# A fused attention and mixer kernel: some score products in plain fp32, without split q and k, and a new order of steps

## Chip, cores and metric

The kernel runs on one core of one Trainium2 chip. The metric is the device time of one execution in microseconds. Its engines are TensorE (matrix products and transposes), VectorE, ScalarE, GpSimd, and SyncE, which issues the loads; they run side by side, each in the order of its own instructions, and wait for each other by semaphores. In the profile they are PE (PEld for the loading of a product's stationary operand), DVE, ACT, POOL and SP.

## What is computed

Three parts in a row, all in fp32: causal attention over 2 batches of 12 heads (448 positions, head dimension 64), a mixer over positions and channels, and a block with a two-dimensional Fourier transform, a normalization and a two-layer product.

```python
scores = np.matmul(q, k.transpose(0, 1, 3, 2)) / np.sqrt(64)
scores = np.where(np.triu(ones, k=1), -1e9, scores)
attn = np.exp(scores - scores.max(-1, keepdims=True))
attn = attn / (attn.sum(-1, keepdims=True) + 1e-9)
x = merge_heads(np.matmul(attn, v))                      # (2, 448, 768)
u = x + (np.maximum(x.T @ w_tok1, 0) @ w_tok2).T         # over positions
x = u + np.maximum(u @ w_ch1, 0) @ w_ch2                 # over channels
u = x + np.real(np.fft.fft(np.fft.fft(x, axis=1), axis=2))
out = u + np.maximum(normalize(u) @ m2_ch1, 0) @ m2_ch2
```

## The kernel before

**Precision.** Most products multiply numbers that are split in two: a value rounded to the short form fp32r ("high") and the rest ("low"). A product of two split operands is three passes of fp32r, high by high, high by low, low by high. Transposes and the product of P with V are in plain fp32, which TensorE does as two instructions for each product.

**Attention.** The 24 heads are worked in 12 pairs; pair n holds two heads on partitions 0 to 63 and 64 to 127, and the two products of a pair (e = 0 and 1) use one half of the array's rows each. The 448 query rows are 4 blocks of 112; block i needs only the first 112 (i + 1) keys, and the widths were rounded up to 256 at least. Blocks 0 and 1 of a pair share a group (g = 0), blocks 2 and 3 are the groups 1 and 2. After a group's products, four small bf16 products add the causal mask (-1e9 above the diagonal).

**Steps and engines.** `ORDER` is a list of words; each word is one step, and the order of the words is the order of the instructions on every engine, so a word's place decides what stands ahead of it in its own engine's queue. Nothing is reordered at run time: a step that waits holds all later steps of its engine. The letters (pair n, and a part after a point):

- K: the loads of raw k and q (SyncE, two each); V: load of v; R: load of a raw weight (float64 words).
- k, l: kh and kl, the split of k (ScalarE; GpSimd, for pair 0 VectorE). q, m: qh (q times 0.125, ScalarE) and ql (VectorE).
- S n.g: score products of a group with its masks (TensorE). N n.i: the negated row maxima (nmx, VectorE). E n.i: the exponentials, two activations, each with a read of the row sum (ScalarE).
- T n.u: the transposes of P (TensorE), C n.u: their copy out of PSUM (pt; ScalarE for u = 1 and 3, else VectorE); P: P times V; O: its copy (ScalarE); X: transposes back (TensorE).
- Z: row sum plus 1e-9 and its reciprocal (`divisors`, VectorE, tiles of 112 x 8); x: the division (VectorE). h, g: the split of the result (ScalarE, GpSimd).
- A, r, s and D, d: the mixer over positions for three pairs at a time; B, b: transposes of x and their copy; u, w: the split of the result.
- W k.j: step j of converting raw weight k; W0 and W1 are w_tok1 (tiles w1h, w1l) and w_tok2, step 5 is the subtraction for the low part on GpSimd. U, y, z, Y, a: the first channel products.

**Buffers.** PSUM has 8 banks. Banks 0 to 3 are the ring of `ybank` (transposes, P times V, mixer), banks 4 to 7 are two pairs for scores (`spair`). A step that takes a bank waits until the last readers of what was in it are done. Raw q and k are loaded into tiles of `resid` that are free at this time, 6 of them for the first 5 pairs, later 3 (`stage`); a load waits until the last reader of the tile is done.

**Start.** Seven products of a constant with itself (`mean_w`) keep TensorE working until the first scores.

Of the kernel before, what the change touches and what calls it, by code (L numbers as in the profile page):

```python
# [70 lines left out]
ORDER = """K0 k0 l0 K1 q0 m0 S0.0 N0.0 N0.1 S0.1 N0.2 S0.2 k1 l1 N0.3 q1 m1 E0.0 E0.1 S1.0 N1.0 N1.1 K2 E0.2 S1.1 E0.3 T0.2 T0.0
N1.2 C0.2 k2 q2 E1.0 T0.1 T0.3 C0.0 T0.4 E1.1 l2 m2 S1.2 E1.2 S2.0 N1.3 V1 V0 C0.3 N2.0 C0.4 C0.1 P0 R0 W0.0 W0.1 N2.1
K3 K4 E1.3 k3 T1.0 T1.2 S2.1 T1.1 C1.0 O0 T1.4 T1.3 C1.2 X0 E2.0 q3 E2.1 N2.2 E2.2 S2.2 l3 m3 S3.0 C1.1 k4 Z0 x0 N2.3
C1.3 q4 C1.4 P1 N3.0 E2.3 T2.0 T2.3 T2.4 N3.1 S3.1 R1 W1.0 O1 T2.2 W0.2 m4 C2.0 B0.0 C2.3 T2.1 C2.4 X1 E3.0 E3.1 S3.2
N3.2 E3.2 l4 S4.0 V3 V2 b0.0 C2.1 C2.2 P2 W0.3 W0.4 W0.5 N3.3 N4.0 Z1 x1 N4.1 K5 q5 E3.3 T3.0 C3.0 T3.1 T3.2 Z2 O2
T3.4 k5 C3.2 C3.1 B0.1 X2 T3.3 E4.0 E4.1 S4.1 S4.2 C3.4 W1.1 b0.1 h0 C3.3 P3 l5 g0 N4.2 N4.3 E4.2 m5 S5.0 E4.3 S5.1 x2
T4.3 Z4 W1.2 Z3 T4.4 C4.4 O3 h1 T4.1 h2 T4.0 C4.3 T4.2 C4.0 C4.2 N5.0 X3 K6 C4.1 k6 N5.2 N5.1 B0.2 g2 g1 R2 W2.0 q6
A0.1 A0.0 x3 V5 V4 W1.3 W2.1 E5.0 E5.1 S5.2 l6 m6 E5.2 S6.0 W1.4 K7 r0.0 N5.3 P4 E5.3 S6.1 N6.0 N6.1 s0.0 r0.1 b0.2
T5.4 O4 k7 s0.1 X4 T5.1 T5.0 C5.4 T5.2 E6.0 E6.1 x4 W1.5 D0.0 C5.1 D0.1 N6.2 C5.0 T5.3 W2.2 S6.2 E6.2 q7 h3 l7 m7 S7.0
d0.1 C5.2 K8 q8 C5.3 P5 N6.3 R3 k8 h4 N7.0 E6.3 N7.1 d0.0 T6.4 T6.2 T6.0 E7.0 E7.1 S7.1 S7.2 O5 T6.3 l8 g4 V6 K9 C6.3  # L80
k9 C6.2 C6.4 B1.1 X5 C6.0 T6.1 D0.2 N7.2 m8 q9 Z5 x5 N7.3 W2.3 b1.1 B1.2 C6.1 B1.0 P6 Z6 d0.2 E7.2 S8.0 N8.0 N8.1 h5
E7.3 T7.3 O6 b1.2 T7.0 b1.0 T7.2 C7.3 T7.4 T7.1 C7.0 X6 E8.0 E8.1 S8.1 S8.2 C7.1 W2.4 Z7 g5 g3 C7.2 A1.1 C7.4 A1.0 x6
N8.2 B2.0 N8.3 W3.0 W3.1 W3.2 E8.2 l9 m9 S9.0 E8.3 S9.1 V7 P7 V8 K10 r1.1 s1.1 u0.1 h6 W2.5 Z8 u0.0 r1.0 s1.0 N9.0
T8.0 W3.3 T8.1 b2.0 T8.3 q10 u0.2 k10 R4 W4.0 N9.1 E9.0 O7 X7 C8.1 C8.0 T8.4 E9.1 C8.3 D1.0 x7 B2.1 T8.2 N9.2 S9.2 m10
E9.2 l10 w0.1 S10.0 C8.4 d1.0 C8.2 P8 b2.1 N9.3 E9.3 T9.2 T9.1 D1.1 W3.4 O8 h7 K11 q11 T9.0 W4.1 N10.0 N10.1 W4.2 C9.2
T9.3 C9.1 T9.4 E10.0 C9.3 E10.1 d1.1 X8 C9.0 D1.2 S10.1 S10.2 m11 x8 h8 k11 C9.4 V9 P9 V11 Z9 u1.0 N10.2 E10.2 N10.3
E10.3 d1.2 O9 W3.5 l11 S11.0 S11.1 B2.2 R5 W5.0 b2.2 T10.1 C10.1 T10.0 T10.2 g7 g8 w0.2 w0.0 g6 N11.0 N11.2 N11.1
T10.3 C10.3 u1.2 E11.0 A2.0 r2.0 C10.2 C10.0 X9 T10.4 W4.3 A2.1 W5.1 x9 W5.2 W4.4 E11.1 S11.2 s2.0 V10 C10.4 P10 N11.3
u1.1 E11.2 r2.1 s2.1 E11.3 T11.2 C11.2 T11.0 C11.0 T11.1 O10 T11.4 T11.3 W5.3 C11.4 X10 W4.5 R6 W6.0 W6.1 Z10 R7 C11.1
C11.3 P11 w1.2 D2.0 O11 X11 x10 D2.2 d2.2 Z11 x11 h10 d2.0 B3.1 b3.1 u2.0 h9 W5.4 w1.1 w1.0 U0 g10 B3.2 U1 W6.2 u2.2  # L90
y0 b3.2 h11 B3.0 y1 W5.5 W7.0 W7.1 W6.3 W6.4 g9 g11 A3.0 A3.1 z0 D2.1 b3.0 r3.0 s3.0 W7.2 z1 W7.3 r3.1 s3.1 U2 y2 D3.0
D3.1 d3.0 z2 d3.1 W7.4 U3 D3.2 y3 u3.1 W6.5 W7.5 w2.2 w2.0 d2.1 u3.0 u2.1 w3.0 w3.1 w2.1 z3 Y0 a0 d3.2 Y1 a1 u3.2 w3.2
"""


# [5 lines left out]
def fused_kernel(ctx: ExitStack, tc: tile.TileContext, qk, v, w1, w2, wa, wb, wc, wd, fa, fb, out):  # L101
# [159 lines left out]
    with ExitStack() as actx:  # L261
# [94 lines left out]
        def maxima(n, i):  # L356
            c = pairs[n]
            if i == 0:
                c.nmx = small(ap, "nmx")
# [2 lines left out]
            if n or g < 2:
                vec.tensor_reduce(  # L363
                    out=c.nmx[:, i], in_=c.sp[g][:TS, :, c0 : c0 + w], axis=AX.X, op=ALU.max, negate=True
                )
            else:
                for e in range(2):
                    vec.tensor_reduce(out=c.nmx[:, i, e], in_=c.se[g][e][:, :w], axis=AX.X, op=ALU.max, negate=True)
# [641 lines left out]
```

## Time and profile before

| | us |
|---|---|
| median of 3 runs | 685.57 |
| fastest and slowest run | 685.55, 686.62 |
| span of the profiled execution | 687.0 |
| busy in it: TensorE, VectorE, ScalarE, GpSimd | 680.4, 534.8, 291.7, 125.5 |

The profile is of one more execution, whose own time is its span, from the first instruction to the last. A row of a time line gives start, length, engine, line, operation, the tiles written and read, shapes, how many instructions were merged into it, and in brackets the idle time before it with what ended it. Lengths of matrix products are modelled and overlap; the distance from one start to the next says what a product really costs.

### The profile page before, as it was taken

To read this page: it belongs to the slowest core of one execution; us is meant where nothing else is said; L and a number is where in the kernel's file an instruction comes from. 1 tells how busy PE (TensorE), PEld (TensorE's weight loads), DVE (VectorE), ACT (ScalarE), POOL (GpSimd) and SP (SyncE) were. 2 spreads that over 40 slices of the span, in tenths; PEclk is the share of its full clock that TensorE was granted. 3 is DMA by queue.
4 is the path that set the end of the run, shared out by engine and by line. 5 is a ranking of instruction groups with operands and counts; after the bars stand their busy time and mean duration, and the time that the engine had idled before them with its cause. 6 is when DMAs were issued, how large, how long until landed. Compare 5 with 4: busy or idle time off the path is not lost.

```text
span 687.0 us, 10288 instructions
## 1 busy us (share of the span) xinstructions
PE 680.4 (99%) x3946; PEld 623.8 (91%) x3946; DVE 534.8 (78%) x885; ACT 291.7 (42%) x624; POOL 125.5 (18%) x106
## 2 busy tenths in 40 slices
...
GB/s 268 68 103 138 91 99 45 49 234 151 125 127 133 111 149 95 93 1 1 92 77 108 123 144 76 120 92 153 93 122 93 155 124 151 93 84 83 108 48 54
...
## 3 DMA queue, kind: packets, MB, share of 16 engines
...
q14 instruction: 18, 0.15, 0.1%
HBM read 69.96 MB, written 2.75 MB: 106 GB/s over the span
## 4 chain that ended last, share of the span: by engine, by line
PE 98%; DVE 1%; DMA 0%; ACT 0%; issue 0%; DVEq 0%
PE psum L247 13%; PE psum L226 13%; PE psum L227 13%; PE psum L252 13%; PE psum L251 13%; PE psum L228 12%; PE psum L340 4%; PE psum L391 4%; PE psum L408 3%; PE psum L472 2%; PE psum L503 2%; PE psum L701 2%; PE psum L770 1%; PE psum L354 1%; PE psum L427 1%; PE psum L490 1%
## 5 line engine op out<-in xcount | busy, mean ns | idle before, releaser
L247 PE MATMUL psum<-gh,wh 128*128 128x448 f32 x432 | 157.4, 364 | 0.0
L226 PE MATMUL psum<-acth,wh 128*128 128x448 f32 x432 | 156.9, 363 | 0.0
L252 PE MATMUL psum<-gl,wh 128*128 128x448 f32 x432 | 156.5, 362 | 0.0
L227 PE MATMUL psum<-acth,wl 128*128 128x448 f32 x432 | 156.4, 362 | 0.0
L251 PE MATMUL psum<-gh,wl 128*128 128x448 f32 x432 | 156.1, 361 | 0.0
L228 PE MATMUL psum<-actl,wh 128*128 128x448 f32 x432 | 155.9, 361 | 0.0
L141 ACT ACTIVATE m<-w 128x512 f32<-128x512 f32 (+2 forms) x92 | 71.0, 773 | 127.4 <-DVE wl L161 83.0
L159 ACT CAST wh<-m 128x512 fp32r<-128x512 f32 (+1 forms) x90 | 63.4, 705 | 91.6 <-PE psum L252 52.1
L252 PEld LDWEIGHTS psum<-gl,wh 128*128 128x128 f32 x432 | 81.0, 188 | 6.4 <-DVE gl L234 0.4
L226 PEld LDWEIGHTS psum<-acth,wh 128*128 128x128 f32 x432 | 81.1, 188 | 5.7
L228 PEld LDWEIGHTS psum<-actl,wh 128*128 128x128 f32 x432 | 80.9, 187 | 5.8
L251 PEld LDWEIGHTS psum<-gh,wl 128*128 128x128 f32 x432 | 80.9, 187 | 5.5 <-issue 0.2
L247 PEld LDWEIGHTS psum<-gh,wh 128*128 128x128 f32 x432 | 81.1, 188 | 5.2 <-issue 0.2
L227 PEld LDWEIGHTS psum<-acth,wl 128*128 128x128 f32 x432 | 81.0, 188 | 4.6
L161 DVE TENSOR_TENSOR wl<-m,wh 128x512 fp32r<-128x512 f32 (+1 forms) x84 | 69.5, 830 | 14.3 <-ACT wh L159 13.9
L143 DVE TENSOR_SCALAR m<-m 128x512 f32<-128x512 f32 (+2 forms) x92 | 49.9, 543 | 38.8 <-ACT m L141 38.3
L148 DVE SCALAR_TENSOR_TENSOR m<-w,m 128x512 uint32<-128x512 uint32 (+2 forms) x92 | 78.5, 853 | 2.1
L152 DVE SCALAR_TENSOR_TENSOR m<-w,m 128x512 uint32<-128x512 uint32 (+2 forms) x92 | 78.2, 850 | 2.0
L232 ACT ACTIVATE gh<-psum 128x448 fp32r<-128x448 f32 x72 | 37.7, 540 | 65.0 <-PE psum L228 64.8
L234 DVE SCALAR_TENSOR_TENSOR gl<-psum,gh 128x448 fp32r<-128x448 f32 x72 | 43.8, 619 | 26.0 <-ACT gh L232 26.0
L378 ACT ACTIVATE p<-psum,nmx 112x112 f32<-112x112 f32 (+3 forms) x96 | 46.5, 503 | 10.6 <-DVE nmx L363 9.4
L144 DVE TENSOR_SCALAR m<-m 128x512 uint32<-128x512 uint32 (+2 forms) x92 | 48.0, 522 | 2.4
...
## 6 DMA issues: line engine op xcount, KB each, us to landing
...
```

The lines of the kernel that those rows point to most:

```text
L141: act.activation(out=m, in_=hi.bitcast(F32), func=AF.Abs)
L143: vec.tensor_scalar(out=m, in0=m, scalar1=F64_MIN, scalar2=F64_MAX, op0=ALU.max, op1=ALU.min)
L148: vec.scalar_tensor_tensor(out=mu, in0=lo, scalar=29, in1=mu, op0=ALU.logical_shift_right, op1=ALU.bitwise_or)
L152: vec.scalar_tensor_tensor(out=mu, in0=hi, scalar=0xC0000000, in1=mu, op0=ALU.bitwise_and, op1=ALU.bitwise_or)
L159: act.copy(wh, m)
L161: low_engine[0].tensor_tensor(out=wl, in0=m, in1=f(wh), op=ALU.subtract)
L226: mm(pb[:, :S], lhsT=lh, rhs=act_h[ct][b], start=ct == 0, stop=False)
L227: mm(pb[:, :S], lhsT=ll, rhs=act_h[ct][b], start=False, stop=False)
L228: tail[0] = mm(pb[:, :S], lhsT=lh, rhs=act_l[ct][b], start=False, stop=ct == NCT - 1).ins
L247: mm(pb[:, :S], lhsT=lh, rhs=gh, start=j + k == 0 and seeded is None, stop=False, skip_group_check=seeded is not None,)
L251: mm(pb[:, :S], lhsT=ll, rhs=gh, start=False, stop=False, skip_group_check=seeded is not None)
L252: tail[0] = mm(pb[:, :S], lhsT=lh, rhs=gl, start=False, stop=j == last and k == nk - 1, skip_group_check=seeded is not None,).ins
```

## The change

1. For pairs 0 and 1, all score products are plain fp32, from the raw k and from q scaled by 0.125 in place on VectorE (step e, two halves of 224 columns each; part 0 serves blocks 0 and 1). Steps k, l, q and m of these pairs are gone, and their widths are no longer rounded up to 256. Raw q is loaded ahead of k.
2. For pairs 2 to 11, block 0 alone is plain fp32 on 112 columns, from raw k and from a scaled copy of q's first 112 columns (q0, a new step e on GpSimd). Blocks 1 to 3 stay three passes.
3. S0.2 and S1.0 take two neighbouring banks of the `ybank` ring (`ypair`); the maxima of S0.2 become one reduction.
4. The addition in `divisors` becomes a `scalar_tensor_tensor` whose two inputs are both ssum.
5. The warm-up products read a constant 1.0 from the program's own constants; the tile `ones` is smaller.
6. `ORDER` is new throughout.

```diff
-ORDER = """K0 k0 l0 K1 q0 m0 S0.0 N0.0 N0.1 S0.1 N0.2 S0.2 k1 l1 N0.3 q1 m1 E0.0 E0.1 S1.0 N1.0 N1.1 K2 E0.2 S1.1 E0.3 T0.2 T0.0
-N1.2 C0.2 k2 q2 E1.0 T0.1 T0.3 C0.0 T0.4 E1.1 l2 m2 S1.2 E1.2 S2.0 N1.3 V1 V0 C0.3 N2.0 C0.4 C0.1 P0 R0 W0.0 W0.1 N2.1
...
-N3.2 E3.2 l4 S4.0 V3 V2 b0.0 C2.1 C2.2 P2 W0.3 W0.4 W0.5 N3.3 N4.0 Z1 x1 N4.1 K5 q5 E3.3 T3.0 C3.0 T3.1 T3.2 Z2 O2
...
+ORDER = """K0 e0.0 K1 e0.1 e1.0 S0.0 N0.0 N0.1 K2 S0.1 e1.1 S0.2 E0.0 N0.2 S1.0 E0.1 S1.1 E0.2 N1.0 q2 N0.3
+m2 S1.2 N1.2 k2 V1 K3 N1.1 E0.3 E1.2 l2 T0.2 e2 C0.2 Z0 E1.0 T0.4 E1.1 S2.0 V0 T0.0 N1.3 C0.4 E1.3 T0.3 T0.1
+T1.0 C0.0 C0.1 N2.0 C0.3 T1.2 q3 N2.1 K4 E2.1 S2.1 R0 N2.2 P0 E2.0 C1.0 k3 T1.4 Z1 m3 E2.2 C1.2 S2.2 O0 C1.4
...
+C4.2 T4.1 S5.2 C4.0 K6 C4.4 W0.5 h2 C4.3 N5.2 q6 k6 g2 l6 m6 Z3 E5.2 W1.0 V4 C4.1 N5.3 E5.3 B0.1 e6 A0.1 X3
+Z4 W1.1 b0.1 W1.2 W1.3 K7 r0.1 k7 S6.0 P4 A0.0 O4 W1.4 s0.1 B0.2 x3 W1.5 e7 T5.2 l7 q7 N6.1 r0.0 s0.0 T5.1
...
-    ones = const.tile([1, 128], F32, name="ones")
+    ones = const.tile([1, 16], F32, name="ones")
...
+    warm = nc.const_aps.tensor(1.0, [128, 128], F32)
     for _ in range(7):
-        mm(psum[:, 7, :128], lhsT=mean_w, rhs=mean_w, start=True, stop=True)
+        mm(psum[:, 7, :128], lhsT=warm, rhs=warm, start=True, stop=True)
...
+    def ypair():
+        turn["y"] += turn["y"] % 2
+        k = take("y", 4)
+        take("y", 4)
+        return psum[:, k : k + 2]
...
-            c.k32, c.q32 = stage(n), stage(n)
-            nc.sync.dma_start(out=c.k32, in_=qk[b, hp, :, 1])
-            nc.sync.dma_start(out=c.q32, in_=qk[b, hp, :, 0])
+            c.q32, c.k32 = stage(n), stage(n)
+            for t, part in ((c.k32, 1), (c.q32, 0)) if n >= 2 else ((c.q32, 0), (c.k32, 1)):
+                nc.sync.dma_start(out=t, in_=qk[b, hp, :, part])
...
+        def q_first(n, part=0):
+            c = pairs[n]
+            if n < 2:
+                cols = c.q32[:, 2 * TS * part : 2 * TS * (part + 1)]
+                vec.tensor_scalar(out=cols, in0=cols, scalar1=0.125, scalar2=None, op0=ALU.mult)
+                return
+            c.q0 = a1.tile([128, TS], F32, tag="q0", name="q0")
+            pool.tensor_scalar(out=c.q0, in0=c.q32[:, :TS], scalar1=0.125, scalar2=None, op0=ALU.mult)
...
-            if n or g < 2:
-                sp = c.sp[g] = spair()
-                se = c.se[g] = [sp[:TS, e] for e in range(2)]
-            else:
-                se = c.se[g] = [ybank()[:TS] for e in range(2)]
+            sp = c.sp[g] = ypair() if (n, g) in ((0, 2), (1, 0)) else spair()
+            se = c.se[g] = [sp[:TS, e] for e in range(2)]
             for i, c0 in BLOCKS[g]:
-                w = max(256, TS * (i + 1))
-                for m, (qt, kt) in enumerate(((c.qh, c.kh), (c.qh, c.kl), (c.ql, c.kh))):
+                w = max(256 if n >= 2 and i else 0, TS * (i + 1))
+                if n < 2 or i == 0:
+                    passes = ((c.q32 if n < 2 else c.q0, c.k32),)
+                else:
+                    passes = (c.qh, c.kh), (c.qh, c.kl), (c.ql, c.kh)
+                for m, (qt, kt) in enumerate(passes):
...
-            vec.tensor_scalar(out=c.ssum, in0=c.ssum, scalar1=1.0e-9, scalar2=None, op0=ALU.add)
+            vec.scalar_tensor_tensor(out=c.ssum, in0=c.ssum, scalar=1.0e-9, in1=c.ssum, op0=ALU.add, op1=ALU.max)
```

## Rows read from the trace of the kernel before

**Rows 1.** The page: span, and busy time of each engine

```profile
span 687.0 us, 10288 instructions
...
PE 680.4 (99%) x3946; PEld 623.8 (91%) x3946; DVE 534.8 (78%) x885; ACT 291.7 (42%) x624; POOL 125.5 (18%) x106
```

**Rows 2.** Table of stretches: start and end, length, busy time (instructions) by engine

```profile
core 0: us, PE busy (x) PEld busy (x) DVE busy (x) ACT busy (x) POOL busy (x), PEclk, DMA share, GB/s
...
8.00:12.00 4.00, 3.35 (x22) 2.44 (x22) 2.52 (x4) 4.00 (x17) 0.00 (x0) 1.00 1.03 288
...
26.70:34.36 7.66, 7.66 (x82) 6.00 (x81) 7.56 (x12) 7.66 (x24) 0.98 (x1) 1.00 0.41 122
...
119.46:150.00 30.54, 30.54 (x169) 27.83 (x169) 13.46 (x29) 12.45 (x26) 10.73 (x11) 1.00 0.47 157
```

**Rows 3.** Time line of TensorE, 4 to 20 us

```profile
4.54 0.55 PE L340 MATMUL psum<-kh,qh 64*112 64x256 f32 x2
...
5.69 0.41 PE L340 MATMUL psum<-kh,qh 64*112 64x256 f32 x2
...
6.33 0.57 PE L354 MATMUL psum<-maskb,identb 56*112 56x224 bf16 x4
6.59 0.60 PE L340 MATMUL psum<-kh,qh 64*112 64x336 f32 x2
...
11.11 0.56 PE L340 MATMUL psum<-kh,ql 64*112 64x256 f32 x2 [0.65 <-DVE ql L317]
...
13.64 3.90 PE L391 MATMUL psum<-ident,p 112*112 112x112 f32 x20
...
18.25 0.37 PE L340 MATMUL psum<-kh,qh 64*112 64x256 f32 x2
...
19.32 2.11 PE L408 MATMUL psum<-pt,v 112*64 112x448 f32 x16
```

**Rows 4.** Time line of TensorE, 34 to 48 us

```profile
34.36 2.11 PE L408 MATMUL psum<-pt,v 112*64 112x448 f32 x16
36.40 0.98 PE L391 MATMUL psum<-ident,p 112*112 112x112 f32 x8
38.30 0.98 PE L391 MATMUL psum<-ident,p 112*112 112x112 f32 x8 [0.93 <-DVE x L440]
...
44.72 0.28 PE L340 MATMUL psum<-kh,qh 64*112 64x256 f32 x2
...
45.07 0.35 PE L354 MATMUL psum<-maskb,identb 56*112 56x224 bf16 x4
...
45.93 2.13 PE L391 MATMUL psum<-ident,p 112*112 112x112 f32 x20
```

**Rows 5.** Time line of VectorE, near 35 and near 97 us

```profile
35.01 2.27 DVE L420 TENSOR_SCALAR ssum<-ssum 112x8 f32<-112x8 f32 x1
...
97.01 0.95 DVE L148 SCALAR_TENSOR_TENSOR m<-w,m 128x768 uint32<-128x768 uint32 x1
```

**Rows 6.** The instructions of line L420: shortest, median, longest in ns

```profile
L420 DVE TENSOR_SCALAR ssum<-ssum x12: 161/165/2274, 24.6 to 125.2; 112x8 f32<-112x8 f32 x12
```

**Rows 7.** Time line of GpSimd, near 35 and near 97 us

```profile
34.89 2.37 POOL L161 TENSOR_TENSOR w1l<-m,w1h 112x1024 fp32r<-112x1024 f32 x1 [7.20 <-ACT w1h L159]
...
97.38 2.30 POOL L161 TENSOR_TENSOR wl<-m,wh 128x768 fp32r<-128x768 f32 x1 [7.66 <-PE psum L391]
```

**Rows 8.** Groups by line and shape: busy time, mean ns of one, idle before

```profile
L313 ACT ACTIVATE qh<-resid 128x448 fp32r<-128x448 f32 x12 | 7.1, 590 | 0.9 <-PE psum L340 0.9
...
L317 DVE SCALAR_TENSOR_TENSOR ql<-resid,qh 128x448 fp32r<-128x448 f32 x12 | 7.4, 617 | 0.3 <-ACT qh L313 0.3
...
L308 POOL TENSOR_TENSOR kl<-resid,kh 128x448 fp32r<-128x448 f32 x11 | 12.7, 1155 | 34.9 <-ACT kh L304 34.9
```

**Rows 9.** Landing of the second and third load, issued at 1.18 and 1.65

```profile
DMA to landing us min/median/max: 2.7/2.7/2.7
...
DMA to landing us min/median/max: 4.0/4.0/4.0
```

More of the change, by code (lines that the diff above doesn't have):

```diff
@@ L68 @@
 ENGINES = {getattr(mybir.EngineType, e) for e in ("PE", "DVE", "Activation", "Pool", "SP")}
-ORDER = """K0 k0 l0 K1 q0 m0 S0.0 N0.0 N0.1 S0.1 N0.2 S0.2 k1 l1 N0.3 q1 m1 E0.0 E0.1 S1.0 N1.0 N1.1 K2 E0.2 S1.1 E0.3 T0.2 T0.0
-N1.2 C0.2 k2 q2 E1.0 T0.1 T0.3 C0.0 T0.4 E1.1 l2 m2 S1.2 E1.2 S2.0 N1.3 V1 V0 C0.3 N2.0 C0.4 C0.1 P0 R0 W0.0 W0.1 N2.1
-K3 K4 E1.3 k3 T1.0 T1.2 S2.1 T1.1 C1.0 O0 T1.4 T1.3 C1.2 X0 E2.0 q3 E2.1 N2.2 E2.2 S2.2 l3 m3 S3.0 C1.1 k4 Z0 x0 N2.3
-C1.3 q4 C1.4 P1 N3.0 E2.3 T2.0 T2.3 T2.4 N3.1 S3.1 R1 W1.0 O1 T2.2 W0.2 m4 C2.0 B0.0 C2.3 T2.1 C2.4 X1 E3.0 E3.1 S3.2
@@ L75 @@
-N3.2 E3.2 l4 S4.0 V3 V2 b0.0 C2.1 C2.2 P2 W0.3 W0.4 W0.5 N3.3 N4.0 Z1 x1 N4.1 K5 q5 E3.3 T3.0 C3.0 T3.1 T3.2 Z2 O2
[L76 to L89, printed above, removed]
@@ L90 @@
-C11.3 P11 w1.2 D2.0 O11 X11 x10 D2.2 d2.2 Z11 x11 h10 d2.0 B3.1 b3.1 u2.0 h9 W5.4 w1.1 w1.0 U0 g10 B3.2 U1 W6.2 u2.2
-y0 b3.2 h11 B3.0 y1 W5.5 W7.0 W7.1 W6.3 W6.4 g9 g11 A3.0 A3.1 z0 D2.1 b3.0 r3.0 s3.0 W7.2 z1 W7.3 r3.1 s3.1 U2 y2 D3.0
-D3.1 d3.0 z2 d3.1 W7.4 U3 D3.2 y3 u3.1 W6.5 W7.5 w2.2 w2.0 d2.1 u3.0 u2.1 w3.0 w3.1 w2.1 z3 Y0 a0 d3.2 Y1 a1 u3.2 w3.2
+ORDER = """K0 e0.0 K1 e0.1 e1.0 S0.0 N0.0 N0.1 K2 S0.1 e1.1 S0.2 E0.0 N0.2 S1.0 E0.1 S1.1 E0.2 N1.0 q2 N0.3
+m2 S1.2 N1.2 k2 V1 K3 N1.1 E0.3 E1.2 l2 T0.2 e2 C0.2 Z0 E1.0 T0.4 E1.1 S2.0 V0 T0.0 N1.3 C0.4 E1.3 T0.3 T0.1
@@ new lines @@
+T1.0 C0.0 C0.1 N2.0 C0.3 T1.2 q3 N2.1 K4 E2.1 S2.1 R0 N2.2 P0 E2.0 C1.0 k3 T1.4 Z1 m3 E2.2 C1.2 S2.2 O0 C1.4
+l3 V3 T1.1 T1.3 N2.3 q4 C1.1 m4 X0 e3 S3.0 x0 R1 C1.3 W0.0 N3.0 E2.3 P1 e4 T2.2 S3.1 N3.1 T2.1 E3.1 O1 T2.0
+W0.1 E3.0 B0.0 C2.2 S3.2 k4 N3.2 C2.0 K5 l4 W0.2 N3.3 V2 T2.4 C2.1 T2.3 E3.2 X1 b0.0 C2.3 S4.0 C2.4 N4.0 q5
+E3.3 k5 l5 P2 S4.1 T3.0 x1 E4.0 T3.2 O2 T3.1 N4.1 W0.3 N4.2 V5 C3.0 X2 E4.1 C3.2 h0 E4.2 S4.2 C3.1 m5 Z2
+T3.3 C3.3 T3.4 e5 h1 C3.4 S5.0 g0 N4.3 W0.4 E4.3 P3 g1 O3 x2 T4.2 N5.1 E5.1 T4.0 N5.0 T4.3 R2 S5.1 E5.0 T4.4
@@ new lines @@
+C4.2 T4.1 S5.2 C4.0 K6 C4.4 W0.5 h2 C4.3 N5.2 q6 k6 g2 l6 m6 Z3 E5.2 W1.0 V4 C4.1 N5.3 E5.3 B0.1 e6 A0.1 X3
+Z4 W1.1 b0.1 W1.2 W1.3 K7 r0.1 k7 S6.0 P4 A0.0 O4 W1.4 s0.1 B0.2 x3 W1.5 e7 T5.2 l7 q7 N6.1 r0.0 s0.0 T5.1
+N6.0 b0.2 S6.1 m7 T5.3 C5.1 D0.0 C5.2 T5.0 Z5 E6.0 E6.1 K8 N6.2 E6.2 C5.3 d0.0 S6.2 D0.2 N6.3 C5.0 E6.3 T5.4
+q8 X4 S7.2 d0.2 S7.0 k8 C5.4 x4 D0.1 N7.3 T6.0 T6.4 W2.0 P5 N7.0 V6 m8 d0.1 l8 N7.1 T6.3 E7.3 S7.1 h3 h4
+C6.0 W2.1 E7.1 O5 C6.4 e8 T6.1 E7.0 C6.3 C6.1 N7.2 R3 g3 T6.2 E7.2 W2.2 B1.1 S8.2 X5 g4 C6.2 x5 K9 q9 N8.3
@@ new lines @@
+k9 b1.1 h5 P6 E8.3 e9 O6 T7.0 m9 W3.0 S8.1 T7.3 W2.3 g5 C7.0 S8.0 T7.2 N8.2 C7.3 E8.2 B1.2 A1.0 N8.0 T7.1 l9
+C7.2 N8.1 K10 S9.0 r1.0 b1.2 E8.1 C7.1 W3.1 W3.2 s1.0 B1.0 X6 V7 b1.0 N9.0 A1.1 E8.0 S9.1 u0.1 N9.1 Z6 T7.4
+e10 x6 E9.0 C7.4 r1.1 E9.1 W2.4 w0.1 s1.1 W2.5 R4 T8.0 Z7 P7 T8.3 q10 D1.0 Z8 k10 m10 C8.3 C8.0 W3.3 S9.2 O7
+W3.4 X7 B2.0 V8 W4.0 N9.2 d1.0 E9.2 b2.0 D1.2 N9.3 l10 T8.2 E9.3 S10.0 x7 u0.0 T8.4 T8.1 h7 d1.2 D1.1 K11
+k11 N10.1 Z9 q11 C8.1 C8.4 u0.2 l11 w0.2 C8.2 E10.1 N10.0 W3.5 g7 m11 R5 S10.2 h6 T9.0 P8 T9.1 u1.2 d1.1
@@ new lines @@
+E10.0 N10.3 V9 S10.1 C9.0 T9.2 V11 O8 C9.2 E10.3 X8 C9.1 T9.4 x8 S11.1 B2.1 e11 C9.4 N10.2 T9.3 w0.0 h8 w1.2
+C9.3 P9 E10.2 T10.0 b2.1 N11.2 u1.1 T10.1 T10.2 O9 W4.1 C10.0 T10.4 E11.2 S11.0 C10.1 T10.3 S11.2 C10.4 u1.0
+V10 g8 W5.0 C10.2 N11.0 E11.0 W4.2 B2.2 g6 W4.3 Z10 C10.3 N11.1 A2.0 N11.3 E11.1 w1.1 r2.0 W5.1 b2.2 X9 W4.4
+A2.1 r2.1 W5.2 s2.0 w1.0 E11.3 U0 P10 x9 s2.1 R6 W5.3 T11.0 T11.3 O10 T11.2 C11.0 T11.4 X10 C11.3 C11.2 x10
+y0 Z11 T11.1 C11.1 W4.5 W6.0 z0 W5.4 R7 W6.1 D2.2 U2 C11.4 W5.5 P11 W6.2 W7.0 B3.1 d2.2 D2.0 W7.1 D2.1 h10
@@ L93 @@
+W6.3 O11 g10 W6.4 y2 W6.5 X11 z2 h9 b3.1 U1 d2.0 x11 U3 h11 W7.2 d2.1 B3.0 y1 u2.2 y3 z1 g9 g11 A3.1 u2.1
+u2.0 A3.0 b3.0 w2.1 W7.3 B3.2 w2.0 W7.4 W7.5 r3.0 z3 Y0 r3.1 s3.1 b3.2 s3.0 D3.0 d3.0 D3.2 u3.0 d3.2 a0 w3.0
+D3.1 u3.2 w2.2 d3.1 w3.2 u3.1 Y1 a1 w3.1
 """
```

22 lines of the change are left out of this document (8 added, 14 removed).

## The prediction, written before the result was known

> **What bounds the kernel now.** Read the busy times first [rows 1]: TensorE works 680.4 of 687.0 us. So only two things move the end: what TensorE has to do, and the 6.6 us in which it does nothing. The change touches the attention stage alone (to about 150 us), and the table of stretches shows who else is near the limit there [rows 2]: from 26.7 to 34.4 us VectorE works 7.56 and ScalarE 7.66 of 7.66 us, as full as TensorE; from 119 us on both work less than half the time. So early on three engines bind, and later TensorE alone: a microsecond that TensorE gains late is kept, one gained early may be spent waiting for the others.
>
> TensorE's time line shows three losses. First, the first product starts at 4.54 us [rows 3]. Second, the engine runs at half its pace for long: three passes of 256 columns take 0.64 us from 5.69 to 6.33, but 0.35 us from 44.72 to 45.07; 20 transposes last 3.90 us at 13.64 and 2.13 us at 45.93 [rows 3, 4]. Per column and pass that is 1.2 against 2.4 GHz; the scores at 18.25 are already fast, so the full pace begins near 17 us. The column of granted clock shows 1.00 all along [rows 2], so here the starts decide. Third, there are waits: 0.65 us at 11.11 for ql of pair 1 [rows 3], and 0.93 us at 38.30 for x [rows 4]. The second has a curious source: VectorE's addition on 112x8 numbers took 2.27 us at 35.01 [rows 5], where 0.165 is its median [rows 6]. It ended when GpSimd's subtraction for w1l, 34.89 to 37.26, ended [rows 7].
>
> **Block 0 in plain fp32, pairs 2 to 11.** Removed: three passes of 256 columns, 0.35 us at full pace, from 44.72 to 45.07 [rows 4]. Added: one fp32 product per head on 112 columns. The trace has no fp32 score product; the nearest is P times V, fp32 too, two heads side by side: widths 448, 336, 224 and 112, together 1120 columns, in 2.04 us, from 34.36 to 36.40 [rows 4], or 1.82 ns a column for both heads. That gives 112 x 1.82 = 0.20 us, a gain of 0.15 us. There the heads lie side by side in columns of the array, here in rows; if the two heads did not overlap it would be 0.41, a loss of 0.06. I take the gain, since the fp32r passes of two heads do overlap in rows: 256 columns of both heads in 0.117 us is one pass's time at 2.4 GHz, not two. Ten pairs: **-1.5 us** (bounds -1.5 and +0.6).
>
> **q0 on GpSimd.** Ten new instructions of 128x112. No such row; kl on 128x448 with two inputs takes 1.16 us [rows 8]: between a quarter of it, 0.29, and the whole I take 0.35, as one input is less work. GpSimd is busy 0.98 of 7.66 us [rows 2], and each new instruction stands well ahead of its product: 0 while GpSimd keeps up. Where it does not, the wait is in the term for new waits.
>
> **Pairs 0 and 1: what goes and what comes.** ScalarE loses four conversions of about 0.59, 2.4 us; VectorE loses kl of pair 0 and two ql, 0.62 each, and gains four scalings of 224 columns, each between 0.165 (the 112x8 addition) and 0.62 (ql, twice the columns and two inputs); I take 0.25, so VectorE is 0.9 us freer. GpSimd loses one kl [rows 6, 8]. One reduction of S0.2 replaces two: hidden.
>
> TensorE now multiplies 1120 columns a pair in fp32: at half pace 1120 x 3.64 ns = 4.08 us plus three sets of masks at 0.26 or less (6.33 to 6.59 [rows 3]), say 0.6: 4.7 us a pair. The first score needs q, k and one scaling. The first load is now q, ahead of k; the second, issued at 1.18, lands 2.7 us later, at 3.9 [rows 9], and the scaling lies between. The warm-up starts perhaps 0.2 us sooner, since its constant needs no VectorE. So the start is 4.0 for 4.54. Both pairs' scores then run on without waits for ql, on banks that are free when their turn comes: 4.0 + 9.4 = 13.4 us. With the transposes of pair 0 at half pace, 3.9, it is 17.3 us. Before, the same work (scores of both pairs, transposes of pair 0) ended at 18.25 [rows 3]. That is -1.0 us, if the full pace begins no sooner than before.
>
> If it begins sooner, ScalarE binds. From 8 to 12 us it does 17 instructions in 4.00 us, 16 of them one pair's exponentials and their reads [rows 2]: 3.8 us a pair, two pairs 7.6; q2 and k2 1.2, two copies about as much as conversions, 1.1: 9.9 us. The new order puts e1.0 ahead of N0.0 on VectorE; it waits for q of pair 1, issued at 1.65 and landing 4.0 later, at 5.65 [rows 9]; behind it queue the maxima and so the exponentials. These begin near 6.3, so the product P0 cannot come before 16.2, against 19.32 [rows 3]. It then has some 1.5 us more TensorE work done before it (two groups of transposes and S2.1 now stand ahead of it), so at most -4.6. Between -1.0 and -4.6 I take **-2.0 us**, nearer the first, because right behind it VectorE and ScalarE are full [rows 2].
>
> The new order also puts N1.0 ahead of N0.3, so E0.3, and T0.2 after it, wait for S1.0. At half pace S1.1 and S1.2 cover that; at full pace some of it shows, and that is in the bound. Loads: K3 must now wait for S0.2 (TensorE itself reads pair 0's raw q and k), and V0, K4 and R0 queue behind it on SyncE. S0.2 ends near 8.7 and P0 comes 8 us later; a load under this traffic lands in 4.0 [rows 9]: covered. W0.0 moves further down the order than R0 does. If that cover failed, P0 would slip by the lateness of V0, a microsecond or two.
>
> **The wait at 38.30.** W0.5, the w1l subtraction, is moved to the end of pair 4, and the 112x8 addition becomes a scalar_tensor_tensor. After W0.5 the next transposes that need VectorE (T5.2) have A0.1, P4 and A0.0 ahead of them, over 6 us of TensorE work, to hide a blocked VectorE. So the wait goes: **-0.9 us** (bounds -0.9 and 0).
>
> The row shows one block of 2.27 us beside one GpSimd instruction [rows 5, 7]. The Trainium skill, "SBUF — State Buffer", section "Who interferes with whom", says that VectorE in a two-port mode, or with two SBUF inputs against a GpSimd instruction that reads SBUF, blocks or is blocked wholly. The new form has two SBUF inputs (ssum twice), so by that rule it can be blocked as the old one was, and the sum would be 683.6 if it met an uncovered place. The trace does not decide it: L148, which has two SBUF inputs, ran 0.95 us from 97.01, and the wl that GpSimd began inside it took 2.30 us, but VectorE came first there [rows 5, 7].
>
> **New waits.** The whole order is rewritten. Bounds: 0, and 4 us, about 1 us for each of four long subtractions like the one of 2.30 [rows 7] that could hold VectorE at a bad moment as w1l did. The two waits that the old order has, 0.65 and 0.93, are the nearest measure; with three engines equally full I take **+1.5 us**.
>
> **Sum.** -1.5 - 2.0 - 0.9 + 1.5 = -2.9 us. The span profiled is 687.0 us, 1.4 above the median run (685.57) and 0.4 above the slowest; the sum is a difference, and I set it against the median: **682.7 us**.
>
> **Rivals.**
> 1. *The gain goes under in VectorE and ScalarE.* For it: both full at 26.7 to 34.4 [rows 2]. TensorE comes early and waits at each group of transposes; the start's 2.0 shrinks to 0.5, new waits grow to 2.5: -1.5 - 0.5 - 0.9 + 2.5 = -0.4, 685.2 us. Against: both have 0.9 to 2.4 us less to do by then.
> 2. *The block stays.* GpSimd holds the 112x8 addition, in its new form too, at a place without cover, for 0.9 us as before: 683.6; twice: 684.5. For it: [rows 5, 7]; against: the long cover after W0.5.
> 3. *The full pace comes early.* The scores run without a gap from 4.0 us, where before there was a break of 0.65 at 11.11. Start -4.0 in place of -2.0: 680.7 us.
> 4. *The two heads don't overlap in fp32* (slower). Each pair's products at half pace take 8.2 us for 4.1, two pairs 8.2 more; some 2 of it would be spent waiting for exponentials anyway: start +4.2 instead of -2.0, block 0 +0.6 instead of -1.5: 691.0 us. It decides once a 112-column block of two heads takes over 0.35 us at full pace. Against it: P times V [rows 4].
>
> **Chances.** Forecast with the single block of rival 2 (681.2 to 684.2) 0.52; rival 3 0.15; rival 1, or rival 2 twice, 0.23, most of it within 0.2% of 685.57; rival 4, or rival 1 with worse waits, 0.10. A difference of 0.2%, 1.4 us, is about what this measurement can tell. Faster 0.67, same 0.23, slower 0.10. The range takes in rival 1 on one side and most of rival 3 on the other: 680.2 to 686.2.
>
> **What would show it.** First score product near 4.0 us; the last of pair 1 done by 13.4 or sooner; no wait for ql of pair 1. An fp32 block 0 of 0.20 us for both heads from pair 2 on. No 2 us instruction in the divisors. TensorE idle under 1.5 us between 20 and 130 us. Wrong if fp32 blocks take 0.4 us, if TensorE's starts are still slow well past 17 us, or if several waits for nmx, pt or x of 0.5 us and more stand ahead of transposes.

## The result, and the profile after

The changed kernel takes 694.37 us (median of 4 runs, 693.38 to 695.24), the one before 685.56 (4 runs, 685.25 to 686.62): the ratio is 1.0126, 95% interval 1.0112 to 1.0140. It is 8.8 us slower; 682.7 was forecast. Two of its four executions, the profiled one among them, show a granted clock of 0.995 over the whole span (695.24 and 694.98 us), the other two 1.000 (693.76 and 693.38).

The page of the profiled execution (its own time 695.24), beside [rows 1]:

```profile
span 693.5 us, 10231 instructions
...
PE 683.5 (99%) x3910; PEld 620.1 (89%) x3910; DVE 541.7 (78%) x885; ACT 290.3 (42%) x620; POOL 133.4 (19%) x115
```

TensorE issues 36 products fewer, and is busy 3.1 us longer. So the loss is not in what it has to multiply but in how long its products take, and in waits. The time line of TensorE, as in [rows 3]:

```profile
4.01 1.01 PE L360 MATMUL psum<-resid,resid 64*112 64x112 f32 x8
...
9.71 0.96 PE L360 MATMUL psum<-resid,resid 64*112 64x336 f32 x3 [1.92 <-ACT p L392]
...
13.11 1.74 PE L405 MATMUL psum<-ident,p 112*112 112x112 f32 x8
...
16.45 2.89 PE L405 MATMUL psum<-ident,p 112*112 112x112 f32 x20
...
20.02 2.11 PE L422 MATMUL psum<-pt,v 112*64 112x448 f32 x16
```

The first score is at 4.01, and pair 1's scores end at 13.1, both as forecast. But 1.92 us are lost at 9.71 on an exponential. ScalarE and VectorE show why:

```profile
7.16 1.28 ACT L392 ACT_TABLE_LOAD   x1 [7.16 <-DVE nmx L382]
8.45 0.35 ACT L392 ACTIVATE p<-psum,nmx 112x112 f32<-112x112 f32 x1
```

```profile
5.96 0.28 DVE L333 TENSOR_SCALAR resid<-resid 128x224 f32<-128x224 f32 x1 [2.04 <-DMA resid<-in_qk]
6.16 0.92 DVE L382 TENSOR_REDUCE nmx<-psum 112x2 f32<-112x224 f32 x2
```

The maxima wait behind e1.0 for q of pair 1, as forecast; but ScalarE then loads a table of 1.28 us, because the first exponential is now its first instruction of all. Behind the wait comes half pace, in the table of stretches (columns as in [rows 2]; 1.00 of the granted clock is 2.4 GHz, 0.50 is 1.2):

```profile
8.00:12.00 4.00, 2.29 (x13) 1.66 (x14) 1.68 (x4) 3.99 (x16) 0.00 (x0) 0.91 0.52 163
12.00:16.00 4.00, 4.00 (x26) 3.02 (x24) 3.31 (x7) 3.88 (x17) 1.61 (x2) 0.50 0.44 129
16.00:20.00 4.00, 4.00 (x36) 3.50 (x32) 2.09 (x5) 2.72 (x8) 0.00 (x0) 0.74 0.70 211
```

The same product of transposes that later takes 0.1 us takes 0.21 at 13.11. Later there are several waits where before had one, at 38.30 [rows 4]; the table of waits of TensorE (releaser; us in total, times, longest):

```profile
PE psum L360 <- ACT p L392: 1.9, 1, 1.9
PE psum L405 <- DVE pt L414: 1.2, 2, 0.6
PE psum L405 <- DVE x L454: 0.9, 1, 0.9
PE psum L441 <- DVE pt L414: 0.8, 1, 0.8
```

The fp32 block 0 itself does what it should; time line of TensorE at 25.6, for pair 3, beside [rows 4]:

```profile
25.59 0.45 PE L360 MATMUL psum<-resid,q 64*112 64x112 f32 x4
25.81 0.35 PE L360 MATMUL psum<-kh,qh 64*112 64x256 f32 x2
```

Both heads take 0.22 us, from start to start.

**TensorE's time by kind of work.** I sum the distances from one start to the next over each kind, from the first P times V to the end; "changes" counts the steps between score or mask products (64 or 56 rows of the array) and any other work; "waits" sums what such a distance exceeds its usual value by, where that is over 0.25 us, up to 130 us. Each is of one execution; the numbers ahead of the names are those of the experiments below.

| kernel | median us | first P times V at | changes | waits |
|---|---|---|---|---|
| before | 685.6 | 19.3 | 34 | 1.1 |
| the change | 694.4 | 20.0 | 54 | 4.5 |
| 1: change, old order | 694.8 | 16.6 | 34 | 6.3 |
| 2: new order, split scores | 694.8 | 17.4 | 54 | 5.6 |
| 3: change, early table | 692.3 | 16.8 | 54 | 4.5 |
| 6: change, old order, six tiles | 683.9 | 16.6 | 34 | 0 |
| 9: 3 with four waits mended | 691.1 | 17.0 | 54 | 3.3 |
| 10: 9 with joined scores | 701.1 | 16.9 | 38 | 9.9 |
| 11: change, old order, table | 683.4 | 14.5 | 34 | 0.4 |
| 12: 11 with parted scores | 687.6 | 15.3 | 54 | 1.9 |

The new order has 20 changes more; the expectation of run 1 reckoned with 31. From before to after, the kinds change by (waits included): scores -1.5 us, masks +2.2, transposes of P +2.4 though there are 8 fewer (they stand ahead of P0 now, as do six score products and four masks of S2.1), transposes of x +1.0, the rest +1.7.

### The profile page after: what moved, and what is told of

Read it like the earlier page. It is cut to its first block, busy times and chain, and to the rows that moved or that the text cites. A ratio compares the mean times of both kernels' runs of the same rounds, so it can differ in the third digit from the quotient of the medians.

```text
span 693.5 us, 10231 instructions
## 1 busy us (share of the span) xinstructions
PE 683.5 (99%) x3910; PEld 620.1 (89%) x3910; DVE 541.7 (78%) x885; ACT 290.3 (42%) x620; POOL 133.4 (19%) x115
## 4 chain that ended last, share of the span: by engine, by line
PE 96%; DVE 1%; ACT 1%; DMA 1%; issue 0%; SPq 0%; DVEq 0%; ACTq 0%
PE psum L257 13%; PE psum L237 13%; PE psum L262 12%; PE psum L261 12%; PE psum L236 12%; PE psum L238 12%; PE psum L405 4%; PE psum L360 3%; PE psum L422 3%; PE psum L486 3%; PE psum L715 2%; PE psum L517 2%; PE psum L784 1%; PE psum L441 1%; PE psum L504 1%; DMA resid<-in_qk 1%
## 5 line engine op out<-in xcount | busy, mean ns | idle before, releaser
L151 DVE SCALAR_TENSOR_TENSOR m<-w,m 128x512 uint32<-128x512 uint32 (+2 forms) x92 | 80.1, 871 | 2.3
L155 DVE SCALAR_TENSOR_TENSOR m<-w,m 128x512 uint32<-128x512 uint32 (+2 forms) x92 | 79.6, 866 | 1.9
L164 DVE TENSOR_TENSOR wl<-m,wh 128x512 fp32r<-128x512 f32 (+1 forms) x84 | 69.5, 830 | 14.8 <-ACT wh L162 14.5
L147 DVE TENSOR_SCALAR m<-m 128x512 uint32<-128x512 uint32 (+2 forms) x92 | 51.1, 556 | 2.7
```

The lines of the kernel that those rows point to most:

```text
L147: vec.tensor_scalar(out=mu, in0=mu, scalar1=3, scalar2=0x3FFFFFF8, op0=ALU.logical_shift_left, op1=ALU.bitwise_and)
L151: vec.scalar_tensor_tensor(out=mu, in0=lo, scalar=29, in1=mu, op0=ALU.logical_shift_right, op1=ALU.bitwise_or)
L155: vec.scalar_tensor_tensor(out=mu, in0=hi, scalar=0xC0000000, in1=mu, op0=ALU.bitwise_and, op1=ALU.bitwise_or)
L164: low_engine[0].tensor_tensor(out=wl, in0=m, in1=f(wh), op=ALU.subtract)
```

## The experiments

The expectations weigh three theories. A: the new order costs the time (the engines' queues and the changes on TensorE). B: the plain fp32 products do. C: the late load of ScalarE's table does.

**1. The change's code in the order of before.** In it the ql of pair 8 is made from a tile that already holds k of pair 9.

```diff
-ORDER = """K0 e0.0 K1 e0.1 e1.0 S0.0 ...
+ORDER = """K0 e0.0 e0.1 K1 S0.0 N0.0 N0.1 S0.1 N0.2 S0.2 e1.0 e1.1 N0.3 ... q2 e2 ...
-  sp = ypair() if (n, g) in ((0, 2), (1, 0)) else spair()
+  sp = ypair() if (n, g) == (0, 2) else spair()
```

> The change's score products in plain fp32, its reordered q and k loads, its new divisors and warm-up, but the steps in the old order and pair 1's first scores in the old banks (the e steps stand where k, l, q, m of pairs 0 and 1 stood, and right behind each q for the later pairs). Theory A, the new order costs the time (31 more changes between score products and other work on TensorE after the first P times V, about 0.1 us each, and some 4 us of new waits): this kernel keeps the fp32 gain of about 0.15 us in each of ten pairs and none of that cost, 683 to 686 us. Theory B, the fp32 products cost the time: 690 us or more. Theory C, the late start of ScalarE costs it (its table load now stands right before the first exponential): up to 3 us over theory A, 686 to 689.

694.84 us, ratio 1.0117 (1.0100 to 1.0134). By the time alone the order would cost nothing. The trace says otherwise: its fourth P times V is at 37.8 us, where that of before was at 42.2, and then it loses the lead to late loads: 4.1 us against run 6 up to the seventh P times V (there qh of pair 8 waits 3.45), and 6.7 more up to the ninth, at qh of pair 10. TensorE near 90 us, ScalarE at 63 and 89, SyncE's queue at 84, and the table of stretches:

```profile
92.90 1.10 PE L443 MATMUL psum<-ident,ots 128*112 128x128 f32 x4 [3.94 <-ACT ots L432]
```

```profile
62.78 0.58 ACT L325 ACTIVATE qh<-resid 128x448 fp32r<-128x448 f32 x1 [3.45 <-DMA resid<-in_qk]
...
88.92 0.58 ACT L325 ACTIVATE qh<-resid 128x448 fp32r<-128x448 f32 x1 [3.85 <-DMA resid<-in_qk]
```

```profile
83.83 0.82 SPq L311 DMA_DIRECT2D resid<-in_qk  x2
```

```profile
91.42:98.24 6.82, 5.34 (x22) 4.88 (x22) 3.15 (x5) 4.75 (x17) 1.31 (x2) 0.50 0.13 35
```

Raw q and k of pair 10 (the expectation of run 6 says 8) are issued only at 83.83. Of the three tiles, the change gives pair 10's k the one of pair 9's q, whose last reader, m9, runs from 83.07 to 83.69; the code before gave it the one of pair 8's q. The last of them arrives 5 us later; qh of pair 10 waits for it, everything behind it on ScalarE waits too (the copy `ots` among it), and TensorE falls to half pace. So the change's swap of the two tiles costs late loads in the old order. In the change's own order it does not: there only the two scalings of the start wait for a load of raw q or k (4.3 us together).

**2. The new order with the scores of before.** Here the load of pair 5's q overwrites k of pair 4 ahead of l4.

```diff
-ORDER = """K0 k0 l0 K1 q0 m0 S0.0 ...
+ORDER = """K0 k0 l0 K1 q0 m0 S0.0 N0.0 N0.1 K2 S0.1 k1 l1 q1 m1 S0.2 ... (the change's order)
   passes = (c.qh, c.kh), (c.qh, c.kl), (c.ql, c.kh)
```

> The new order and its banks, but all scores in three passes of split q and k as before (k, l, q, m for pairs 0 and 1 are back at the places of the e steps, no q0). Theory A: slower than before by the changes between kinds of products (3 us) and the waits (some 4 us), 690 to 695 us. Theory B: within 1.5 us of before. Theory C: within 2 us of before, since the table load is early again.

694.83 us, ratio 1.0125 (1.0110 to 1.0140). The order alone, without one fp32 score, costs as much as the whole change. Its waits stand at the places of the change's: 0.8 at 21.2, 1.0 at 55.3, 0.7 at 71.0, 0.9 at 92.9. One more, 1.1 at 31.0, is this run's own: kl of pair 4 waits for the load that overwrites its input.

**3. The change with the table loaded early.**

```diff
     vec.memset(eps_t, EPS)
+    early = const.tile([128, 16], F32, name="early")[:, :1]
+    act.activation(out=early, in_=eps_t, func=AF.Exp)
```

> The changed kernel with one more activation on one column of a constant as the first work of ScalarE, so that its table is loaded while the first loads are on their way. Theory C: the exponentials start 1.3 us sooner, the 1.9 us wait of TensorE at 7.8 us shrinks to under 1 and the half pace from 11 to 18 us goes: 4 us or more faster than the changed kernel, 690.5 us or less. Theory A: only 1 to 2.5 us faster, 692 to 693.5 us, the rest of the loss stays behind 20 us.

692.33 us, ratio 1.0090 (1.0075 to 1.0105): 2.0 us of the 8.8. The table now loads at 0.73, the first exponential starts at 6.95 and not at 8.45, the wait at 9.71 and the half pace behind it are gone, and P0 is at 16.85. The waits after 20 us are what they were, 4.5. That is what theory A said. ScalarE's first rows:

```profile
0.73 1.28 ACT L126 ACT_TABLE_LOAD   x1 [0.73 <-PEq L1013]
2.02 0.20 ACT L126 ACTIVATE early<-eps_t 128x1 f32<-128x1 f32 x1
6.95 0.35 ACT L394 ACTIVATE p<-psum,nmx 112x112 f32<-112x112 f32 x1 [4.72 <-DVE nmx L384]
```

**4 and 5. Thirty tiny products in the transposes of before, on half and on all rows.**

```diff
+  if n >= 2 and u in (0, 1, 3) and col == 2 * TS:
+      rows_ = slice(0, TS // 2)      # 5: slice(0, TS)
+      mm(tv[:TS, S : S + 32], lhsT=identb[rows_, 0], rhs=maskb[rows_, 0, 0, :32],
+         start=True, stop=True, skip_group_check=True)
```

> The kernel before, with one more tiny bf16 product (56 rows, 32 columns, into columns of the bank that nobody reads) in the middle of 30 groups of transposes, so 60 more changes between the half-array score kind of product and transposes. If a change costs about 0.1 us (theory A): 60 x 0.1 + 30 x 0.03 = 7 us slower, 692 to 693 us. If changes are free and only the product's own time counts: 1 to 1.5 us slower, 686.5 to 687.5.

> The kernel before with the same 30 tiny products inside its transposes as in the run with half rows, but reading all 112 rows of the array in place of 56. If what the half-row products cost (8.7 us, 0.29 each) is the change of the array between half rows and full rows, these cost little more than their own pass, 0.02 to 0.06 us each: 687 to 688.5. If any product of another kind (bf16 after fp32, a product after a transpose) costs it: 693 or more.

Half rows: 694.98 us (1.0140; 1.0108 to 1.0172), +8.7. All rows: 688.22 (1.0038; 1.0025 to 1.0050), +2.2. The time line of TensorE, half rows first:

```profile
43.74 0.40 PE L391 MATMUL psum<-ident,p 112*112 112x112 f32 x2
44.08 0.22 PE L397 MATMUL psum<-maskb,identb 56*112 56x32 bf16 x1
44.23 0.98 PE L391 MATMUL psum<-ident,p 112*112 112x112 f32 x8
```

```profile
44.45 0.18 PE L397 MATMUL psum<-maskb,identb 112*112 112x32 bf16 x1
44.48 0.57 PE L391 MATMUL psum<-ident,p 112*112 112x112 f32 x4
```

A product of 32 columns on all rows is followed 0.03 us later; on half rows 0.15 later, and the transposes before it take 0.34 for two, where two take 0.2. By the times it is (8.7 - 2.2) / 60 = 0.11 us for each change between half and full rows (0.07 to 0.17 by the two intervals). The kernel's own products have the same price: between a transpose and a score 0.189 us (median), between two transposes 0.096; between the last mask and other work 0.140, and 0.025 when another score follows.

**6 and 7. The change in the old order, with six tiles for raw q and k; the same with the early table.** The late pairs' loads go to tiles in which the mixer keeps x, so its last part works on other numbers.

```diff
-  return resid[staged[0] % 6 if n < 5 else 3 + staged[0] % 3][1]
+  return resid[staged[0] % 6][1]
   (ORDER: e9 behind S8.0; 7: the two added lines of run 3)
```

> The change's code with the order of before as in the first run, but raw q and k rotate through six tiles throughout (they had three from pair 5 on), and e9 stands behind S8.0. If the first run lost its time to the late loads of pair 8 (a wait of 4.1 us at 88.7 and the half pace after it, 3.4) and the new order is what costs in the change, this gives 681 to 685. If plain fp32 scores cost the time whatever the order, 690 or more.

> As the run with six tiles, and one exponential of a constant ahead of everything on ScalarE, so that the load of its table (1.28 us) falls under the first loads. If the late table costs with this order what it cost with the new one: 2 us less than the run beside it, 679 to 683. If the table's load only delayed an engine that had time: no difference.

683.95 us (0.9969; 0.9959 to 0.9979) and 683.1 (0.9961; 0.9949 to 0.9974). With the late load gone the same code in the old order gains 2.1 us: the rival, fp32 as the cost, has fallen. The table is worth 0.85 here, less than the 2 expected: in this order e1.0 does not hold the maxima up, and no half pace follows. P0 does come 2.1 us sooner (14.5 for 16.6); the rest is given back behind it.

**8. Before with the new form of the divisors' addition.**

```diff
-  vec.tensor_scalar(out=c.ssum, in0=c.ssum, scalar1=1.0e-9, scalar2=None, op0=ALU.add)
+  vec.scalar_tensor_tensor(out=c.ssum, in0=c.ssum, scalar=1.0e-9, in1=c.ssum, op0=ALU.add, op1=ALU.max)
```

> The kernel before with the new form of the divisors' addition alone (scalar_tensor_tensor, ssum twice). If the new form can be held by GpSimd as the old one was: an addition of 2 us and more at 35 us and the wait for x near 38 stay, 685.6 to 686.9. If not: all twelve additions take under 0.6 us, the wait of 0.9 is gone, 684.6 to 686.

685.87 us (0.9999; 0.9989 to 1.0008): nothing. The rows that answer to [rows 5, 7, 4], of VectorE, GpSimd and TensorE:

```profile
32.61 2.31 DVE L420 SCALAR_TENSOR_TENSOR ssum<-ssum 112x8 f32<-112x8 f32 x1
```

```profile
32.51 2.39 POOL L161 TENSOR_TENSOR w1l<-m,w1h 112x1024 fp32r<-112x1024 f32 x1 [7.23 <-ACT w1h L159]
```

```profile
35.94 0.98 PE L391 MATMUL psum<-ident,p 112*112 112x112 f32 x8 [0.95 <-DVE x L440]
```

**9. Run 3 with four waits mended by moving words.**

```diff
-... T1.4 Z1 m3 E2.2 C1.2 S2.2 O0 C1.4 ...          +... T1.4 E2.2 C1.2 S2.2 O0 C1.4 Z1 m3 ...
-... B0.1 e6 A0.1 X3 Z4 W1.1 b0.1 ... A0.0 ... B0.2 x3 ... b0.2 ...
+... B0.1 B0.2 e6 A0.1 X3 Z4 x3 W1.1 b0.1 b0.2 ... A0.0 ...
-... C6.0 W2.1 E7.1 O5 C6.4 ...                     +... C6.0 E7.1 O5 C6.4 W2.1 ...
-... m10 C8.3 C8.0 ...                              +... C8.3 C8.0 m10 ...
```

> The change with the early table, and six words moved within its order, each for one wait of TensorE that the run with the early table showed: Z1 and m3 behind the copies of pair 1's P (wait of 0.75 at 20.7), B0.2 and its copy ahead of X3 and x3 ahead of w2's conversion (1.02 at 53.1), W2.1 behind C6.4 (0.76 at 68.7), m10 behind C8.0 (0.85 at 90.6, where ql took 1.89 beside GpSimd's subtraction). If those four waits are part of the loss as they stand: 3.4 less than 692.3, 688.9; if other work is late in their place: 691 or more.

691.08 us (1.0093; 1.0075 to 1.0111): 1.25 gained, not 3.4. The four waits are gone from their places, others are late in their stead: 0.5 at 35.9, 0.7 at 48.8, and the longest, 1.22 at 91.8. That one comes from what made the fourth, the ql of pair 10. VectorE, GpSimd and TensorE of the change show it:

```profile
92.19 1.89 DVE L327 SCALAR_TENSOR_TENSOR ql<-resid,qh 128x448 fp32r<-128x448 f32 x1 [0.92 <-ACT qh L323]
94.01 0.61 DVE L414 COPY pt<-psum 112x448 f32<-112x448 f32 x1
```

```profile
91.76 1.84 POOL L164 TENSOR_TENSOR wl<-m,wh 128x768 fp32r<-128x768 f32 x1 [3.50 <-ACT wh L162]
```

```profile
94.76 0.62 PE L441 MATMUL psum<-ident,ots 128*112 128x128 f32 x4 [0.79 <-DVE pt L414]
```

ql, 0.6 us when alone [rows 8], takes 1.89 beside GpSimd's subtraction, which began first; the copy behind it is late, and TensorE waits. In run 9 the copy stands ahead of this ql, but the ql takes as long, the conversion behind it 1.89 too, and TensorE waits for an addition behind both. VectorE, then TensorE of run 9:

```profile
87.32 0.63 DVE L418 COPY pt<-psum 112x448 f32<-112x448 f32 x1
88.14 1.90 DVE L331 SCALAR_TENSOR_TENSOR ql<-resid,qh 128x448 fp32r<-128x448 f32 x1 [0.19 <-ACT qh L327]
89.96 1.89 DVE L159 SCALAR_TENSOR_TENSOR m<-w,m 128x768 uint32<-128x768 uint32 x1
```

```profile
93.20 0.60 PE L409 MATMUL psum<-ident,p 112*112 112x112 f32 x4 [1.06 <-DVE resid L526]
```

Summed over all VectorE instructions up to 130 us, what they take beyond the shortest of their kind is 6.9 us in the change (ten instructions), 2.5 in before (two), 1.3 in run 11 (two).

**10. Run 9 with score groups moved next to each other.** Group 2 then reads the q of pair 4 in pair 2, the kh of pair 7 in pair 5, and the qh of pair 8 in pair 6.

```diff
 S2.2, S3.2, S4.2, S5.2, S6.2: moved down to stand ahead of S3.0, S4.0, S5.0, S6.0, S7.2 (N n.3 and E n.3 behind them)
 S8.0, S11.2, S10.1: moved up to stand behind S8.1, S11.0, S10.2
```

> As the run with the four waits moved, and eight score groups moved next to another score group, so that TensorE changes 16 times less often between score products (half of the array's rows) and other work. The dummies gave 0.11 us a change (8.7 less 2.2, over 60). If that price holds in this order: 1.7 less than the run beside it, about 687. If a change costs only in the dummies' place: no difference, or more, by new waits behind the moved groups.

701.06 us (1.0223; 1.0209 to 1.0237). Changes fell from 54 to 38, but waits grew from 3.3 to 9.9 us: the fourth block's maxima and exponentials come later by the moved groups, and with them the transposes. So it does not decide the price, for which 687 was expected; here the moved words cost more than they saved.

**11. The change in the old order, early table, tiles that are free.**

```diff
-  return resid[staged[0] % 6 if n < 5 else 3 + staged[0] % 3][1]
+  return resid[staged[0] % 6 if n < 10 else (3, 4, 3, 5)[staged[0] - 21]][1]
   (with the order of run 6 and the two added lines of run 3)
```

> The change's code with the early table in the order of before, with six tiles for raw q and k up to pair 9 and three from there on, so that every load lands in a tile that nobody needs any more. If the late tiles are without cost, as in the run with six tiles throughout: 683.1, 3 us below the kernel before. If pairs 10 and 11 wait for their loads: 684 to 687.

683.45 us (0.9965; 0.9952 to 0.9977): faster than both kernels. P0 is at 14.5 us. Two score groups side by side, and a group followed by P times V, on its time line:

```profile
28.28 0.27 PE L378 MATMUL psum<-maskb,identb 56*112 56x112 bf16 x4
28.38 0.41 PE L364 MATMUL psum<-resid,q 64*112 64x112 f32 x4
...
35.51 0.27 PE L378 MATMUL psum<-maskb,identb 56*112 56x112 bf16 x4
35.70 2.11 PE L426 MATMUL psum<-pt,v 112*64 112x448 f32 x16
```

The same four masks take 0.10 us ahead of a score and 0.19 ahead of other work.

**12. Run 11 with ten pairs of neighbouring score groups parted.**

```diff
-... X0 ... S2.2 l3 m3 S3.0 ...        +... S2.2 X0 l3 m3 S3.0 ...
-... T3.3 E4.0 E4.1 S4.1 S4.2 ...      +... E4.0 E4.1 S4.1 T3.3 S4.2 ...
 (X1, A0.0, T5.3, T6.0, X6, B2.0, T8.2, D1.2 likewise behind S3.2, S5.2, S6.2, S7.1, S8.1, S9.0, S9.2, S10.1)
```

> The fastest version (the change's code and the early table in the order of before, 683.4) with ten of its pairs of neighbouring score groups parted by one group of full-row products that stood just ahead of them. TensorE then changes 20 times more often between half rows and full rows, as the new order does some 22 times. If a change costs the 0.11 us that the dummies gave: 2.2 more, 685.6, plus waits that the trace would show. If the price belongs to the dummies alone: 683.4, plus such waits.

687.57 us (1.0023; 1.0013 to 1.0032), 4.1 above run 11. The kinds that see the changes take 2.3 us more (masks 1.5, transposes back 0.4, fp32 blocks 0.2, transposes of P 0.1, of x 0.1), against 2.2 expected; the rest of the 4.6 between the two profiled executions is new waits (1.9 for 0.4) and a P0 that is 0.8 later. So the price holds for the kernel's own steps.

## Why the prediction was wrong

**Block 0, -1.5: right.** 0.22 us for both heads; with the old order the scores of nine pairs behind P0 are 1.45 (run 6) and 1.55 us (run 11) shorter than before. (In the change's own 1.5 are the six products of S2.1, 0.55 us, that only moved ahead of P0.) Rival 4 (heads that do not overlap) is out; the widths of P times V were the right row to go by.

**The start, -2.0: wrong, in three ways.** Its landmarks came (4.01, 13.1), yet P0 is at 20.0. First, "P0 cannot come before 16.2" left out the table load, which [rows 3] hides: before, ScalarE's first instruction came while the loads ran. With it moved back, P0 is at 16.85 (run 3). Second, the half pace that followed the wait at 9.71 was not thought of; the text asked only when the full pace begins, not whether it can be lost. Both are worth 2.0 us together, by run 3; the granted clock of 1.000 in two of the change's executions suggests that there the pace was kept, but neither has a trace. Third, the measure was bad: [rows 3] is of an execution that ran at half pace to 17 us. Run 8, with the same start, has P0 at 16.99 in a span of 684.9, run 4 at 16.29. The own time of an execution is not its span, as was said ahead of the prediction, but lies 1.7 us above it (695.24 and 693.5 for the change), so a median run of before has a span near 683.8, where the one profiled had 687.0. Of the 54 executions of before beside the experiments, 50 have spans of 683.4 to 685.1 and four of 686.8 to 687.1. The difference was worked out against that late execution and set against the median, so most of the gain stood on time that most executions do not lose. What the term measured: less the 1.5 us of work moved ahead of it, P0 stands at 18.5, where the start of before has 16.3 to 17.0 in runs 4, 5 and 8. That is 1.5 to 2.2 us lost, not 2.0 gained. With the early table (run 3) the same reckoning gives 0.9 to 1.6 gained.

**The wait at 38.30, -0.9: gone, by the move of W0.5 that was named.** Beside W0.5, now at 43.04 to 45.42, VectorE has one reduction of usual length and then idles. The new form of the addition had no part in it: run 8, with W0.5 in its old place, keeps a 2.31 us addition and a wait of 0.95. The Trainium skill, "SBUF — State Buffer", section "Who interferes with whom", says that a VectorE instruction with two inputs in SBUF contends with a GpSimd instruction that reads SBUF; run 8 agrees, with 2.31 us against a median of 0.159.

**New waits, +1.5 (0 to 4): mis-sized.** 4.5 us after P0, beyond the bound, at four long places and three short ones. The mechanism named for the bound was right for one (the ql of 1.89 us); in one x3 overwrites what B0.2 has to read first, and B0.2 stands late (1.0); two are copies that stand behind a weight's conversion or the divisors on VectorE. TensorE's idle time from 20 to 130 us, which was to be under 1.5, is 3.5 us (before 1.0).

**The step that is missing: changes between half and full rows.** The prediction counted products and waits, and took the order of TensorE's own steps as free. The old order puts score groups in pairs, the new one parts nearly all: 54 changes for 34, at 0.104 us (half of 0.093 + 0.115) makes 2.1 us; runs 4, 5 and 12 show the price. The Trainium skill, "TensorEngine Tiling (Array Packing)", section "Key Properties", says that a change of the tiling mode drains TensorE, with no price. The runs show a price at each change; whether a drain is behind it, none shows.

**The sum.** The change in its own order lies 10.4 us above the same code in the old order (run 6). Of this, 4.5 are waits as counted in the trace (mending four of them gave back 1.25), 2.1 changes, and some 1.2 the late table and lost pace beyond what they cost in the old order (2.0 less 0.85). The remaining 2.6 are not settled: part is a start that is later for other reasons (P0 of run 3 is 2.3 us behind that of run 7 or 11, with about 1.5 us more work ahead of it, by 8 transposes, 6 score products and 4 masks fewer behind it), the rest many gaps under 0.25 us, which no run took apart. Rival 1 was right in kind (gains spent in waits on VectorE and ScalarE) and far too small. Rival 2 was right in kind too: the new addition takes up to 1.13 us in the change, and at 22.77 one of 0.52, beside a GpSimd subtraction, stands ahead of the copy that TensorE waits for at 24.62 (0.54); the longest block, 0.8 of wait, fell on a ql, not on an addition.
